# Attention with two gated layers on one core: conversion buffers moved into idle attention tiles, unit 8 eight positions later

## The chip, the core and the metric

The program runs on one core of a Trainium2 chip. The metric is device time in microseconds (us) of one execution. The core has five instruction streams: TensorE (PE; its weight loads stand apart as PEld), VectorE (DVE), ScalarE (ACT), GpSimd (POOL) and SyncE (SP), which here issues every DMA. SBUF is the on-chip memory that tiles live in, PSUM the one that TensorE writes.

## The reference, cut to what matters

```python
# q, k, v: [4, 8, 576, 64]; out_d attends over means of 4 rows, out_local over rows nearer than 4
out_d = sm_attn(q_d, k_d, v_d)
out_up = np.repeat(out_d, 4, axis=2)
mask = np.abs(pos[:, None] - pos[None, :]) < 4
scores = np.where(mask, scale * np.matmul(q, k.transpose(0, 1, 3, 2)), -1e9)
x = out_up + np.matmul(softmax(scores), v)            # then [2304, 512]
x = (silu(x @ w_gate) * (x @ w_val)) @ w_out          # d_ff = 1536
h = x @ w_in                                          # d_ff = 2048
out = (np.maximum(h, 0) + alpha * np.minimum(h, 0)) @ w_out2
```

The weights are handed over as 64-bit floats and are read as pairs of 32-bit words.

## The kernel before, in words

**Attention** is cut into 32 units (n = 0 to 31): four pairs of heads for each of eight blocks of 288 tokens. A unit transposes q and k (`a_T`), multiplies the scores into PSUM (`a_QK`, L335), takes the exponential and normalises (`a_EXP`, `a_NRM`; L419 transposes the local weights into a block-diagonal tile `bd`), and multiplies with v (`a_PV`, L431). The sum goes through ACT (L454), DVE (`xf`, L455), ACT (`xh`, L459) and POOL (`xl`, L460) into a high and a low half. The first layer's products of a block read `xh` and `xl` of its four units, the last unit's in the last three of the twelve products of a column tile. v is first copied in DRAM into overlapping windows (`stage`, L250: tensor `vwin`), from which `a_load_w` reads. Units 0 to 7 (`NPRO=8`) come ahead of the first layer's loop, the others are spread over it.

**Weights.** The first layer has 12 column tiles j, each with three slots g, v and o (gate, value, out). `w_load` (L100) brings a raw tile of 512 KB into a slot of pool `wp`; `w_split` (L124) converts it and writes the result, two 32-bit halves, into the same slot. A conversion is an ACT pass (L129), a second ACT pass on the top bytes (L137), a DVE pass (L139) that joins both, an ACT rounding (L142) and a subtraction for the low half (L143, on POOL here). It needs two scratch tiles, `st` and `sk`. Before, the first 30 conversions take both from three slots that rotate, o10, g11 and v11 (`st_slots`, L160); the last six take `st` from pool `hp_` and have no `sk`: then two DVE passes (L131, L132) stand in for L137 and L139.

**Slots shared with attention.** The slots of j = 4 to 11 first hold tiles of units 0 to 7 (`pslot`, L162): q and v of units 0 to 3 in g4 to g5, their work tiles `qs` in v5 to v6, their k in o6 to o7 (then q and v of units 4 to 7), `vd` in g8 to g9 (then `qs` of units 4 to 7; unit 7 has g9), and the block-diagonal tiles of units 0 to 3 in v9, o9, g10 and v10. Units 4 to 7 use those same four again. A raw tile can be loaded only when its slot's last reader is done.

**Order.** Each engine executes a fixed order that a list scheduler has worked out beforehand: program order is the priority, and of what it believes ready the first by priority is taken, also far ahead of its place. `tc.issue_after(x)` puts instructions behind x in their queue. The queue of SP is in order: a DMA that waits holds up those behind it.

**The loop** goes over 8 blocks and 12 column tiles, i = 12 blk + j. For each i it has gate products (`m_g`), value products (`m_v`) and out products of the i before (`m_y`), twelve matmuls each; after each of the three stands a position, 3i, 3i+1, 3i+2, at which steps of attention are hung (`at`, L724). Unit n of 8 and more multiplies its scores at p = OFF + 9(n - 8) and its values at p + 11 (L746 to L752), with OFF = 25. The loads of j = 4 to 9 and of unit 8 are placed ahead of the loop (L713 to L716), those of j = 10 and 11 and the copies `stage(2)`, `stage(3)` in block 0 when the tenth column tile has been handed to conversion (L773 to L779); `stage(2)` and `stage(3)` stand behind the DMA of o11, whose slot nothing else uses, `stage(1)` and unit 8's loads behind that of o7.

Of the kernel before, what the change touches and what calls it, by code (L numbers as in the profile page):

```python
# [8 lines left out]
F32 = mybir.dt.float32  # L9
# [7 lines left out]
DRAM = bass.MemoryType.DRAM  # L17


K = dict(kdP=0, qdP=0, dnP=2, ldn=9, lo='asvw0123', NPRO=8, c=5, a1=1, a2=0, OFF=25, oT=3, oE=3, oP=5, oV=11, vd1=2, vd2=1, pre=(1, 1, 0, 0), lo1=0, lo2=1, nst=3, nrm=0, sub=0, nrm1=0, sub1=0, qtA=0, ldw=1, xl1=0, ly=4, l2=3, st2=2, early=1, w2p=1, la=0, bdV=0, sp=9, s2=0, s3=0, gj=7, gs=1, vr=0, kc=0, gD=(0, 0, 0, 0, 0, 0), gP=(0, 2, 8, 8, 0, 0), gA=(0, 0, 0, 0, 0, 0))  # L20


@with_exitstack
def attn_moe_moe2_kernel(
# [13 lines left out]
    nc = tc.nc  # L38
    B, H, S, D = q.shape
# [6 lines left out]
    NP = H // 2  # L46
# [69 lines left out]
    def st_tile():  # L116
        c = stc[0]
        stc[0] += 1
        if c >= 3 * NEARLY:
            return stp[0].tile([128, 512], F32, tag="st", name="st", bufs=stn[0]), None  # L120
        t = wp.tile([128, 2, 512], F32, tag=st_slots[c % len(st_slots)], name="st2")
        return t[:, 0], t[:, 1]

    def w_split(slot, eng):  # L124
        t = raw.pop(slot)
# [23 lines left out]
    kds = {}  # L149
    vss = {}  # L150
    vds = {}
    bds = [ap_.tile([128, 2, NW, 128], F32, name=f"bd{i}", bufs=1) for i in range(NBD)]

    def coords(n):
        blk, hp = divmod(n, NP)
# [1 line left out]
        return b, half, hp, blk  # L157

    order = [f"{kind}{j}" for j in range(F1 - 8, F1) for kind in "gvo"]
    st_slots = order[5 * NP:][:K["nst"]]  # L160
    NEARLY = F1 - 2
    pslot = {(what, n): order[4 * i + n] for i, what in enumerate(("qv", "qs", "kn", "vd", "bd")) for n in range(NP)}  # L162
    for n in range(NP):
        pslot["qv", n + NP] = pslot["kn", n]
        pslot["qs", n + NP] = pslot["qs" if K["vr"] else "vd", n]
    NPRO = K["NPRO"]
    srs = [ap_.tile([128, 8], F32, name=f"sr{i}", bufs=1) for i in range(4)]

# [25 lines left out]
    def a_load(n):  # L194
        b, half, hp, blk = coords(n)
        h0, t0 = 2 * hp, half * HB
        d = hu[n] = {}
        if n >= NPRO:

            loads = [("qn", q, HB, t0)]  # L200
            if half == 0:
                loads.insert(0, ("kn", k, S, 0))
            for tag, src, rn, r0 in loads:
                t = d[tag] = ap_.tile([128, rn], F32, tag=tag, name=tag, bufs=1)
                for i in range(4):
                    nc.sync.dma_start(
                        out=t[32 * i:32 * (i + 1)].rearrange("r (m c) -> r m c", c=32),
                        in_=src[b, h0 + i // 2, r0:r0 + rn, 32 * (i % 2):32 * (i % 2 + 1)].rearrange("(m r) c -> r m c", r=32))
            return
        if half == 0:  # L210
            kn = d["kn"] = at_(n, [QB, 6, 2, D], "kn")
            for h in range(2):
                nc.sync.dma_start(out=kn[:, :, h], in_=k[b, h0 + h].rearrange("(r p) c -> p r c", p=QB))
        t = at_(n, [128, 2 * NW * 2 * D], "qv").rearrange("p (a w h c) -> p a w h c", a=2, w=NW, h=2)
        d["vw"] = t[:, 1]
        qn = d["qn"] = t[:QB, 0]
        for h in range(2):
            nc.sync.dma_start(out=qn[:, :, h], in_=q[b, h0 + h, t0:t0 + HB, :].rearrange("(r p) c -> p r c", p=QB))
# [18 lines left out]
    def a_load_w(n):  # L237

        b, half, hp, blk = coords(n)
        if n < NP:  # L240
            pbd[n] = at_(n, [128, 2, NW, 128], "bd")
            (nc.vector if K["bdV"] else nc.gpsimd).memset(pbd[n], 0.0)
        if n >= NPRO:
            hu[n]["vw"] = ap_.tile([128, NW, 2, D], F32, tag="vw", name="vw", bufs=NVW)
        t = hu[n]["vw"]
        for h in range(2):
            w0 = ((b * H + 2 * hp + h) * 2 + half) * NW * 128
            nc.sync.dma_start(out=t[:, :, h], in_=vwin[w0:w0 + NW * 128, :].rearrange("(w p) c -> p w c", p=128))
# [143 lines left out]
    def a_NRM(n):  # L392
        d = hu[n]
        sm, loc, sr = d["sm"], d["loc"], d["sr"]
        s4 = sr[:, 0:6].rearrange("p (h w) -> p h w", h=2)
        if not d["la"]:
            nc.vector.tensor_reduce(out=s4, in_=loc, axis=AX.X, op=ALU.add)
        if not d["act"]:
            nc.vector.reduce_sum(sr[:72, 6:8], sm[:72, :, LW:SW], axis=AX.X)
        nc.vector.tensor_scalar_add(out=sr, in0=sr, scalar1=1e-9)  # L400
        nc.vector.reciprocal(out=sr, in_=sr)
        nrm = K["nrm1" if n < NPRO else "nrm"]
        if nrm == 2:
            for h in range(2):
                for w in range(NW):
                    nc.scalar.mul(out=loc[:, h, w], in_=loc[:, h, w], mul=sr[:, NW * h + w:NW * h + w + 1])
        else:
            (nc.vector if nrm else nc.gpsimd).tensor_tensor(out=loc, in0=loc, in1=s4.unsqueeze(3).to_broadcast([128, 2, NW, SWIN]), op=ALU.mult)
        dn = n < 2 * NP and K["dnP"]
        if dn == 2:  # L410
            for h in range(2):
                nc.scalar.mul(out=sm[:72, h, LW:SW], in_=sm[:72, h, LW:SW], mul=sr[:72, 6 + h:7 + h])
        else:
            (nc.gpsimd if dn else nc.vector).tensor_tensor(out=sm[:72, :, LW:SW], in0=sm[:72, :, LW:SW],
                                in1=sr[:72, 6:8].unsqueeze(2).to_broadcast([72, 2, SD]), op=ALU.mult)
        d["bd"] = pbd[n % NP] if n < NPRO else bds[n % NBD]
        for i in range(NS):
            ps = slice(SWIN * i, SWIN * (i + 1))
            nc.vector.transpose(out=d["bd"][ps, :, :, SWIN * i:SWIN * (i + 1)], in_=loc[ps])  # L419
# [62 lines left out]
    def load1(j):  # L482
        for kind in "gvo":
            w_load(kind, j, f"{kind}{j}")
# [145 lines left out]
    if True:  # L630
# [26 lines left out]
                                fill=NEG, base=SUB + 2, channel_multiplier=0)  # L657
        for i in range(NS):
            nc.gpsimd.tensor_copy(mask[SWIN * i:SWIN * (i + 1)], tmp[:, :, i])
        for t in bds:  # L660
            nc.gpsimd.memset(t, 0.0)
        pstack = ExitStack()
        pgv = pstack.enter_context(tc.tile_pool(name="pgv", bufs=1, space=PSUM))
        P = [ATT, Y[0], Y[1], pgv.tile([128, 2, 512], F32, name="gv")]
# [39 lines left out]
            a_all(n, P[n % NP % 3])  # L704
        preps(K["pre"][3])
        def load8():
            if B > 1:
                stage(1)
            a_load(NPRO)
            a_load_v(NPRO)  # L710
            a_load_w(NPRO)

        for j in range(4, F1 - 2):  # L713
            load1(j)
        with tc.issue_after(wdma[f"o{K['gj']}"]):
            load8()  # L716
        for b in range(2, B):
            if K["gs"] == 0:
                stage(b)
        nc.sync.dma_start(out=alpha_sb, in_=alpha.rearrange("(j p) -> p j", p=128))  # L720

        ev = {}
# [1 line left out]
        def at(pos, fn):  # L724
            ev.setdefault(pos, []).append(fn)

        def a_pre(n):
            a_T(n, ATT)
            a_vd(n)
            if n + 1 < NHU:  # L730
                a_load(n + 1)
                a_load_v(n + 1)
# [4 lines left out]
                a_load_w(n + 1)  # L737

        OFF = K["OFF"]
        at(0 if NPRO == NP else OFF - 7, lambda: a_pre(NPRO))  # L740
        for n in range(NPRO, NHU):
            if n < 2 * NP:
                c = K["c"]
# [15 lines left out]
        for i, (blk, j) in enumerate(fts):  # L759
            if blk == NB1 - 1 and j == 0:  # L760
                assert not ev, ev.keys()
                astack.close()
                side2 = ctx.enter_context(tc.tile_pool(name="p2a", bufs=1, side="right"))
                stp[0] = side2
                attstack.close()
                pa2 = ctx.enter_context(tc.tile_pool(name="pa2", bufs=1, space=PSUM, side="right"))
                HT += GV[0], GV[1], *[pa2.tile([128, 512], F32, name=f"h{e}") for e in range(2)]
                stn[0] = K["st2"]
            if blk == 0:
                while pc[0] <= min(j + K["early"], F1 - 1):  # L770
                    prep1(pc[0])
                    pc[0] += 1
                    if pc[0] == NEARLY:  # L773
                        load1(F1 - 2)
                        load1(F1 - 1)
                        if K["gs"]:
                            with tc.issue_after(wdma[f"o{F1 - 1}"]):
                                for b in range(2, B):
                                    stage(b)  # L779
            m_g(blk, j)  # L780
            run(3 * i)
            m_v(blk, j)
            run(3 * i + 1)
            if i > 0:
                m_y(*fts[i - 1])
            run(3 * i + 2)
            if blk == NB1 - 1:
                load2(j)
                if j >= K["l2"]:
                    prep2(j - K["l2"])  # L790
                if j == K["ly"]:
                    load_y(0)
# [52 lines left out]
```

## Time and profile before

| | us |
|---|---|
| median of 3 runs (1015.98 to 1018.08) | 1017.56 |
| the profiled execution | 1017.97 |
| its span, first to last instruction | 1015.9 |
| TensorE busy in the span | 969.7 |
| ScalarE, VectorE, GpSimd busy | 306.8, 478.9, 383.5 |

The profiled execution has 2.1 us around its span. The matmuls of a column tile follow each other every 0.13 us, although each is shown with 0.29 us, since they overlap. Idle time of TensorE is what to look for; the clock that it was granted stands beside it, as a share of 2.4 GHz.

### The profile page before, as it was taken

What the parts mean: (1) busy time and instruction counts of PE and PEld (TensorE: products, weight loads), DVE (VectorE), ACT (ScalarE), POOL (GpSimd) and SP (SyncE); (2) the same over time, 40 slices, a digit from 0 to 9 for tenths busy, and PEclk for the clock granted to TensorE, in tenths of its full rate; (3) what the DMA queues carried; (4) which work ended last, traced back from release to release, by engine and by line L of the source; (5) the groups of instructions that cost most, each with busy time, mean ns of one, the idle gap of its engine ahead of it and who ended that gap; (6) DMA issues with size and microseconds to landing.
All of it is one profiled execution on the core that took longest, in us unless ns stands there. A gap on an engine that the chain in (4) does not pass through costs nothing.

```text
span 1015.9 us, 19233 instructions
## 1 busy us (share of the span) xinstructions
PE 969.7 (95%) x7760; PEld 865.3 (85%) x7760; DVE 478.9 (47%) x1015; ACT 306.8 (30%) x690; POOL 383.5 (38%) x492
## 2 busy tenths in 40 slices
PE   5489789999999999999999999999999999999998
PEld 4379679999999999999999998888888888888897
DVE  5577864555444555444532769622222322322232
ACT  3869632222221322222323556312111101211111
POOL 5868763234322344222223435624223322322222
PEclk9999899999999999999999999999999999999999
DMA  8998741132111321110103883102000100100010
GB/s 202 290 315 283 184 93 27 35 73 59 38 46 21 76 50 41 40 26 18 43 9 116 282 254 122 42 1 63 22 0 21 52 1 1 42 11 1 0 43 22
DMA packets 135894, 77.81 MB, mean 77 GB/s; under 512 B 97406, under 2 KB 127102, under 8 KB 135038
## 3 DMA queue, kind: packets, MB, share of 16 engines
q1 hardware_dynamic: 135804, 76.58, 27.0%
q8 instruction: 60, 0.98, 0.4%
q14 instruction: 30, 0.25, 0.1%
HBM read 67.12 MB, written 15.73 MB: 82 GB/s over the span
## 4 chain that ended last, share of the span: by engine, by line
PE 82%; SPq 4%; DVE 4%; DMA 3%; POOL 3%; issue 2%; ACT 2%; POOLq 0%; DVEq 0%; ACTq 0%
PE y L610 7%; PE y L612 6%; PE y L611 6%; PE g L473 6%; PE v L474 6%; PE v L473 6%; PE v L475 6%; PE g L474 6%; PE g L475 6%; PE y L473 4%; PE y L475 4%; PE y L474 4%; PE h L473 3%; PE h L475 3%; PE h L474 3%
## 5 line engine op out<-in xcount | busy, mean ns | idle before, releaser
L598 POOL TENSOR_TENSOR gl<-t,gh 128x512 fp32r<-128x512 f32 (+1 forms) x80 | 97.0, 1214 | 250.9 <-ACT gh L597 244.4
L597 ACT CAST gh<-t 128x512 fp32r<-128x512 f32 (+1 forms) x80 | 46.2, 578 | 278.7 <-DVE t L594 239.2
L473 PE MATMUL g<-xh,w 128*128 128x288 f32 x384 | 117.4, 306 | 10.0 <-DVE u L513 4.4
L475 PE MATMUL g<-xh,w 128*128 128x288 f32 x384 | 115.1, 300 | 1.9 <-POOL w L143 1.8
L473 PE MATMUL v<-xh,w 128*128 128x288 f32 x384 | 116.0, 302 | 0.6 <-ACT w L142 0.4
L474 PE MATMUL v<-xl,w 128*128 128x288 f32 x384 | 115.3, 300 | 0.0
L474 PE MATMUL g<-xl,w 128*128 128x288 f32 x384 | 115.0, 300 | 0.0
L474 PE MATMUL y<-pl,w 128*128 128x288 f32 x384 | 113.8, 298 | 1.3 <-POOL pl L523 1.2
L475 PE MATMUL v<-xh,w 128*128 128x288 f32 x384 | 113.8, 296 | 0.6 <-POOL w L143 0.6
L610 PE MATMUL y<-w,gh 128*128 128x512 f32 x288 | 113.2, 393 | 1.0 <-ACT sy L542 1.0
L475 PE MATMUL y<-ph,w 128*128 128x288 f32 x384 | 113.0, 296 | 0.0
L611 PE MATMUL y<-w,gh 128*128 128x512 f32 x288 | 112.8, 392 | 0.0
L612 PE MATMUL y<-w,gl 128*128 128x512 f32 x288 | 112.0, 392 | 0.0
L513 DVE SCALAR_TENSOR_TENSOR u<-u,g 128x288 f32<-128x288 f32 x96 | 43.3, 451 | 144.1 <-ACT u L512 144.1
L473 PE MATMUL y<-ph,w 128*128 128x288 f32 x384 | 111.0, 301 | 0.2 <-ACT ph L522 0.2
L523 POOL TENSOR_TENSOR pl<-u,ph 128x288 fp32r<-128x288 f32 x96 | 79.8, 832 | 59.4 <-ACT ph L522 58.6
L143 POOL TENSOR_TENSOR w<-st,w 128x512 fp32r<-128x512 f32 x52 | 70.2, 1356 | 60.7 <-ACT w L142 60.5
L473 PEld LDWEIGHTS g<-xh,w 128*128 128x128 f32 x384 | 73.5, 191 | 12.9 <-DVE u L513 5.7
L592 DVE TENSOR_SCALAR t<-h,alpha 128x512 f32<-128x512 f32 (+1 forms) x40 | 27.9, 697 | 110.7 <-PE h L475 109.5
L512 ACT ACTIVATE u<-g 128x288 f32<-128x288 f32 x96 | 39.4, 410 | 122.8 <-PE g L475 121.3
L475 PEld LDWEIGHTS g<-xh,w 128*128 128x128 f32 x384 | 73.7, 192 | 2.7 <-POOL w L143 2.4
L473 PEld LDWEIGHTS v<-xh,w 128*128 128x128 f32 x384 | 72.8, 190 | 2.3 <-DVE u L519 1.0
(190 smaller groups left out, 2143.4 us busy)
## 6 DMA issues: line engine op xcount, KB each, us to landing
raw<-in_moe_w_out_dram SPq DMA_DIRECT2D x28, 512.0 KB
raw<-in_moe_w_in_dram SPq DMA_DIRECT2D x16, 512.0 KB
raw<-in_moe_w_gate_dram SPq DMA_DIRECT2D x12, 512.0 KB
raw<-in_moe_w_val_dram SPq DMA_DIRECT2D x12, 512.0 KB
vw<-vwin SPq DMA_DIRECT2D x48, 96.0 KB
out_dram<-os SPq DMA_DIRECT2D x18, 256.0 KB
sy<-y SPq DMA_DIRECT2D x16, 256.0 KB
y<-ys SPq DMA_DIRECT2D x14, 288.0 KB
```

What stands on the lines that cost most here:

```text
L143: eng.tensor_sub(w[:, 1], st, f32(w[:, 0]))
L473: nc.tensor.matmul(o, lhi, rhi, start=first, stop=False)
L474: nc.tensor.matmul(o, lhi, rlo, start=False, stop=False)
L475: nc.tensor.matmul(o, llo, rhi, start=False, stop=last)
L512: nc.scalar.activation(out=u, in_=GV[0][:, :HB], func=AF.Tanh, scale=0.5)
L513: nc.vector.scalar_tensor_tensor(out=u, in0=u, scalar=1.0, in1=GV[0][:, :HB], op0=ALU.add, op1=ALU.mult)
L523: nc.gpsimd.tensor_sub(pl, u, f32(ph))
L597: nc.scalar.copy(out=gh[:, :n], in_=t[:, :n])
L598: nc.gpsimd.tensor_sub(gl[:, :n], t[:, :n], f32(gh[:, :n]))
L610: nc.tensor.matmul(o, gh[:, ms], ohi, start=(j == 0), stop=False)
L611: nc.tensor.matmul(o, gh[:, ms], olo, start=False, stop=False)
L612: nc.tensor.matmul(o, gl[:, ms], ohi, start=False, stop=(j == F2 - 1))
```

## The change

All 36 conversions of the first layer take `st` and `sk` from the pools of attention and of the first layer: of three conversions in a row the first two use tag `st` of `hp_` (two buffers), the third the tile `bd` of pool `ap_`; `sk` lies in `vd`, `kn` and a new tile `sk` of `ap_`. So slots o10, g11 and v11 are free of scratch, and units 4 to 7 get block-diagonal tiles of their own there and in o11, with a memset each. All raw tiles of j = 4 to 11 are loaded in one row. `load8` (unit 8's block-diagonal tile with its memset, `stage(1)`, unit 8's loads, `stage(2)` and `stage(3)`) is called when the last column tile has been handed to conversion, its DMAs behind that of o11. OFF goes from 25 to 33, the first step of unit 8 from position 18 to 31.

```diff
-K = dict(... OFF=25, ...)
+K = dict(... OFF=33, ...)
...
     def st_tile():
         c = stc[0]
         stc[0] += 1
-        if c >= 3 * NEARLY:
+        if c >= 3 * F1:
             return stp[0].tile([128, 512], F32, tag="st", name="st", bufs=stn[0]), None
-        t = wp.tile([128, 2, 512], F32, tag=st_slots[c % len(st_slots)], name="st2")
-        return t[:, 0], t[:, 1]
+
+        if c % 3 == 2:
+            st = ap_.tile([128, 512], F32, tag="bd", name="st", bufs=1)
+        else:
+            st = hp_.tile([128, 512], F32, tag="st", name="st", bufs=NST)
+        return st, ap_.tile([128, 512], F32, tag=("vd", "kn", "sk")[c % 3], name="sk", bufs=1)
...
-    bds = [ap_.tile([128, 2, NW, 128], F32, name=f"bd{i}", bufs=1) for i in range(NBD)]
+    bds = []
...
-    st_slots = order[5 * NP:][:K["nst"]]
-    NEARLY = F1 - 2
...
         pslot["qs", n + NP] = pslot["qs" if K["vr"] else "vd", n]
+        pslot["bd", n + NP] = order[5 * NP + n]
...
-        if n < NP:
+        if n < NPRO:
             pbd[n] = at_(n, [128, 2, NW, 128], "bd")
             (nc.vector if K["bdV"] else nc.gpsimd).memset(pbd[n], 0.0)
...
-        d["bd"] = pbd[n % NP] if n < NPRO else bds[n % NBD]
+        d["bd"] = pbd[n] if n < NPRO else bds[n % NBD]
...
-        for t in bds:
-            nc.gpsimd.memset(t, 0.0)
...
         def load8():
-            if B > 1:
+            bds.append(ap_.tile([128, 2, NW, 128], F32, tag="bd", name="bd", bufs=1))
+            nc.gpsimd.memset(bds[0], 0.0)
+            with tc.issue_after(wdma[f"o{F1 - 1}"]):
                 stage(1)
-            a_load(NPRO)
-            a_load_v(NPRO)
-            a_load_w(NPRO)
-
-        for j in range(4, F1 - 2):
+                a_load(NPRO)
+                a_load_v(NPRO)
+                a_load_w(NPRO)
+                for b in range(2, B):
+                    stage(b)
+
+        for j in range(4, F1):
             load1(j)
-        with tc.issue_after(wdma[f"o{K['gj']}"]):
-            load8()
...
-        at(0 if NPRO == NP else OFF - 7, lambda: a_pre(NPRO))
+        at(0 if NPRO == NP else OFF - 2, lambda: a_pre(NPRO))
...
                     pc[0] += 1
-                    if pc[0] == NEARLY:
-                        load1(F1 - 2)
-                        load1(F1 - 1)
-                        if K["gs"]:
-                            with tc.issue_after(wdma[f"o{F1 - 1}"]):
-                                for b in range(2, B):
-                                    stage(b)
+                    if pc[0] == F1:
+                        load8()
```

## Rows read from the trace of the kernel before

**Rows 1.** The page, parts 1 and 2: TensorE's busy time; its granted clock.

```profile
PE 969.7 (95%) x7760; PEld 865.3 (85%) x7760; DVE 478.9 (47%) x1015; ACT 306.8 (30%) x690; POOL 383.5 (38%) x492
...
PEclk9999899999999999999999999999999999999999
```

**Rows 2.** Busy time by stretch: engines' us (instructions), granted clock, DMA share, GB/s.

```profile
54.00:69.00 15.00, 10.64 (x203) 8.77 (x202) 13.40 (x40) 10.73 (x33) 11.02 (x19) 0.92 0.98 330
...
66.50:104.00 37.50, 37.44 (x368) 35.87 (x369) 27.93 (x56) 31.39 (x73) 28.65 (x28) 0.95 0.88 296
104.00:118.40 14.40, 11.14 (x121) 9.77 (x120) 12.66 (x21) 10.70 (x22) 11.86 (x12) 0.98 0.75 185
118.40:124.80 6.40, 4.17 (x16) 3.35 (x16) 6.37 (x12) 1.68 (x5) 5.13 (x6) 0.50 0.71 161
124.80:149.00 24.20, 21.23 (x232) 18.65 (x233) 19.40 (x40) 10.40 (x23) 16.50 (x22) 1.00 0.43 91
```

**Rows 3.** Timeline, TensorE: start, length, line, operation; in brackets idle before and releaser.

```profile
106.23 0.40 PE L473 MATMUL g<-xh,w 128*128 128x288 f32 x1 [1.06 <-DVE u L513]
...
118.47 0.61 PE L473 MATMUL g<-xh,w 128*128 128x288 f32 x1 [2.18 <-ACT w L142]
...
121.15 0.61 PE L475 MATMUL g<-xh,w 128*128 128x288 f32 x1 [1.83 <-POOL w L143]
...
137.62 0.40 PE L473 MATMUL v<-xh,w 128*128 128x288 f32 x1 [0.45 <-ACT w L142]
...
140.34 0.40 PE L475 MATMUL v<-xh,w 128*128 128x288 f32 x1 [0.59 <-POOL w L143]
...
143.12 0.40 PE L473 MATMUL g<-xh,w 128*128 128x288 f32 x1 [0.94 <-DVE u L513]
```

**Rows 4.** Timeline, DMA issues of SP: start, and length until the group's last issue.

```profile
55.27 0.52 SPq L257 DMA_DIRECT2D vwin<-in_v_dram  x1
55.89 0.54 SPq L106 DMA_DIRECT2D raw<-in_moe_w_val_dram  x1
...
83.30 12.37 SPq L104 DMA_DIRECT2D raw<-in_moe_w_out_dram  x2
95.73 0.53 SPq L257 DMA_DIRECT2D vwin<-in_v_dram  x1
...
106.35 0.45 SPq L106 DMA_DIRECT2D raw<-in_moe_w_gate_dram  x1
...
121.13 0.35 SPq L104 DMA_DIRECT2D raw<-in_moe_w_out_dram  x1
...
122.92 0.41 SPq L106 DMA_DIRECT2D raw<-in_moe_w_val_dram  x1
```

**Rows 5.** DMA issues by source and size: the large copies of v.

```profile
vwin<-in_v_dram SPq DMA_DIRECT2D x2, 1536.0 KB
```

**Rows 6.** Timeline, ScalarE: first passes of two conversions.

```profile
69.96 0.67 ACT L129 ACTIVATE st<-raw 128x512 f32<-128x512 f32 x1
...
116.27 0.67 ACT L129 ACTIVATE st<-raw 128x512 f32<-128x512 f32 x1
```

**Rows 7.** Timeline, GpSimd: the low half of unit 7's result.

```profile
101.44 1.28 POOL L460 TENSOR_TENSOR xl<-qs,xh 128x288 fp32r<-128x288 f32 x1
```

**Rows 8.** Operations by line: count, ns (min/median/max), first and last start.

```profile
L137 ACT ACTIVATE st<-raw x30: 641/660/697, 28.8 to 116.8; 128x512 int32<-128x512 uint8 x30
...
L242 POOL MEMSET bd<- x4: 738/740/742, 0.9 to 3.2; 128x768 f32 x4
```

**Rows 9.** Timeline: values of units 11 and 12, unit 11's low half, block 2's first product.

```profile
197.03 0.67 PE L450 MATMUL att<-bd,vw 128*64 128x96 f32 x12
...
200.37 0.81 POOL L460 TENSOR_TENSOR xl<-xf,xh 128x288 fp32r<-128x288 f32 x1 [2.19 <-ACT xh L459]
...
209.27 0.30 PE L473 MATMUL g<-xh,w 128*128 128x288 f32 x1
...
213.92 0.67 PE L450 MATMUL att<-bd,vw 128*64 128x96 f32 x12
```

More of the change, by code (lines that the diff above doesn't have):

```diff
@@ L17 @@
 DRAM = bass.MemoryType.DRAM
-K = dict(kdP=0, qdP=0, dnP=2, ldn=9, lo='asvw0123', NPRO=8, c=5, a1=1, a2=0, OFF=25, oT=3, oE=3, oP=5, oV=11, vd1=2, vd2=1, pre=(1, 1, 0, 0), lo1=0, lo2=1, nst=3, nrm=0, sub=0, nrm1=0, sub1=0, qtA=0, ldw=1, xl1=0, ly=4, l2=3, st2=2, early=1, w2p=1, la=0, bdV=0, sp=9, s2=0, s3=0, gj=7, gs=1, vr=0, kc=0, gD=(0, 0, 0, 0, 0, 0), gP=(0, 2, 8, 8, 0, 0), gA=(0, 0, 0, 0, 0, 0))
+K = dict(kdP=0, qdP=0, dnP=2, ldn=9, lo='asvw0123', NPRO=8, c=5, a1=1, a2=0, OFF=33, oT=3, oE=3, oP=5, oV=11, vd1=2, vd2=1, pre=(1, 1, 0, 0), lo1=0, lo2=1, nst=3, nrm=0, sub=0, nrm1=0, sub1=0, qtA=0, ldw=1, xl1=0, ly=4, l2=3, st2=2, early=1, w2p=1, la=0, bdV=0, sp=9, s2=0, s3=0, gj=7, gs=1, vr=0, kc=0, gD=(0, 0, 0, 0, 0, 0), gP=(0, 2, 8, 8, 0, 0), gA=(0, 0, 0, 0, 0, 0))
 @with_exitstack
@@ L706, in load8 @@
         def load8():
-            if B > 1:
+            bds.append(ap_.tile([128, 2, NW, 128], F32, tag="bd", name="bd", bufs=1))
+            nc.gpsimd.memset(bds[0], 0.0)
+            with tc.issue_after(wdma[f"o{F1 - 1}"]):
                 stage(1)
-            a_load(NPRO)
-            a_load_v(NPRO)
-            a_load_w(NPRO)
-        for j in range(4, F1 - 2):
-            load1(j)
-        with tc.issue_after(wdma[f"o{K['gj']}"]):
-            load8()
-        for b in range(2, B):
-            if K["gs"] == 0:
-                stage(b)
+                a_load(NPRO)
[4 more added lines that the diff above has]
+        for j in range(4, F1):
+            load1(j)
         nc.sync.dma_start(out=alpha_sb, in_=alpha.rearrange("(j p) -> p j", p=128))
@@ L772, in attn_moe_moe2_kernel @@
                     pc[0] += 1
-                    if pc[0] == NEARLY:
-                        load1(F1 - 2)
-                        load1(F1 - 1)
-                        if K["gs"]:
-                            with tc.issue_after(wdma[f"o{F1 - 1}"]):
-                                for b in range(2, B):
-                                    stage(b)
+                    if pc[0] == F1:
+                        load8()
             m_g(blk, j)
```

## The prediction

> **What bounds the kernel now.** I read the page first, then busy time by stretch, then the timelines of the engines in the stretches that are not full. TensorE is busy for 969.7 of 1015.9 us and its clock is full but for slices near the start [rows 1], so the time can fall only where TensorE idles or runs at the lower clock. Between 66.5 and 104 us it is full, 37.44 of 37.50 us, and so it is again after 149. What this change can reach lies between: 3.26 us idle up to 118.4, 2.23 up to 124.8, 2.97 up to 149, together 8.46 us; and from 118.4 to 124.8 the clock is 0.50, which is 1.2 instead of 2.4 GHz, so that the 4.17 busy us of that stretch could have been 2.1 [rows 2]. The ceiling is thus 8.46 + 2.1 = 10.6 us.
>
> The timeline names the waits [rows 3]. At 118.47 TensorE has waited 2.18 us for a rounded gate weight, at 121.15 another 1.83 for its low half, then come 0.45, 0.59 and 0.94 us at the end of block 0; 1.06 us at 106.23 waits for DVE. They are waits for conversions, and the DMA queue says why those are late [rows 4]. The first v copy goes out at 55.27, right among the raw tiles, a value tile behind it at 55.89; then two out tiles hold SP from 83.30 to 95.67, since unit 7 still has the slot of the second (o7); a copy and unit 8's loads follow, and only at 106.35 the gate tile that is needed next. That is g9, since its slot holds unit 7's `qs`, which POOL reads until 102.72 [rows 7]; its conversion begins at 116.27 [rows 6]. The last raw tiles, for slots that served as scratch, go out at 121.13 and 122.92 [rows 4], and those are the conversions that the three late waits want.
>
> **The change, part by part.**
>
> *Scratch and raw tiles.* There were three scratch pairs in rotation and there are three now, so the pace is as before: 0. With scratch out of o10, g11 and v11, and the bd tiles of units 0 to 3 no longer held by units 4 to 7, only o7, g9 and o11 still wait for unit 7. All other raw tiles can go ahead of 95 us, in the place of the v copies, which now stand behind o11. The conversions wanted at 137.62, 140.34 and 143.12 then no longer depend on loads at 121 us and later: 0.45 + 0.59 + 0.94 = 1.98 us gone. Bounds: nothing, if conversions are late for want of ScalarE, and the whole 2.97 us idle of that stretch [rows 2]. I take 2.0. What is late next there is ScalarE itself.
>
> *g9.* It still needs unit 7's last read, at 102.72 [rows 7], and so cannot be issued much sooner than that, 3.6 us before its 106.35 [rows 4]. But o11 needs only unit 7's value products, so it comes first, and behind it now go all three copies, not one. Two of them have 1536 KB each [rows 5] and the third is of like size, some 4.6 MB; at the 330 GB/s of the stretch that copied before [rows 2] that is 14 us from 96 on. The value tile issued at 55.89 behind a copy had its first conversion pass at 69.96 [rows 4, 6], 14 us later. So g9 may land at 110 to 113 all the same. What it gains is the work in front of it on ScalarE, since the other conversions are done by then. Its wait and the half clock behind it make 2.18 + 1.83 + 2.1 = 6.1 us. Bounds 0 and 6.1; I take 2.5, nearer to the low end because its load is moved by 3.6 us at most.
>
> The Trainium skill, "DMA: Bandwidth & Descriptors", section "Two DMAs through the same engine are not ordered", says that descriptors of one queue on one engine start in order; by that g9 lies behind all the copies, as the 14 us of that value tile suggest, though no row shows its landing by itself. If small transfers were instead served beside large ones, g9 would land near 105, its 6.1 us would go whole, and the sum would be 1010.9.
>
> *The wait at 106.23*, 1.06 us, comes from DVE behind ScalarE, which is full of conversions: between 0 and 1.06, half taken, 0.5.
>
> *Added work.* Six conversions get a second ACT pass of 0.66 us [rows 8], 4.0 us on ScalarE, in exchange for one of two DVE passes. ScalarE is busy 10.40 of 24.2 us at the end of block 0 [rows 2], which hides it; if the six move ahead of 104, where it is busy 31.39 of 37.5, 4.0 us of delay is what it costs at worst, and then TensorE has its earlier backlog to do. Four memsets come and one moves, 0.74 us each [rows 8], 3 us of POOL, ready from the start; the first conversion pass on top bytes is at 28.8, so they hide in the wait for the first weights. Taken as 0.
>
> *Unit 8.* Its k and v tiles now lie in the last conversions' scratch, so they load some 25 us later than now, right behind the copy at 95.73 [rows 4]. POOL's v sums and the score products queue behind those loads; the block that needs unit 8's group starts near 200, and four units at 17 us each fit. 0 taken, 3 us if TensorE has to stand for it once.
>
> *Eight positions later.* Between the values of units 11 and 12, nine positions, lie 213.92 - 197.03 = 16.89 us [rows 9], so a position is 1.88 us and eight are 15.0. Unit 11's low half is ready at 201.18, block 2's first product starts at 209.27 [rows 9]: 8.1 us to spare before, 6.9 too few after. The first nine products of the tile do not need unit 11, and the second of the last three, which reads the low half, comes 1.3 us after the first; so 5.6 us are to be filled. There is work: nine value products (1.2), the out products of the block before (1.6), unit 11's own values (0.9), score products of the next units (1.0) and transposes (0.6), in sum 5.3. This happens at block 2 to 7, six times; the last has no unit behind it, whose scores would be in the way. Bounds: 0 each, and 5.6 each or 33.6 in all if TensorE filled in nothing. I take 0.3, what is left after filling, five times: 1.5 us. It is nearest to what the timeline shows for the ordinary steps, where values of one unit run inside the products of a block without idle time.
>
> *Sum*, against the profiled execution's 1017.97 (0.41 above the median of the runs): 1017.97 - 2.0 - 2.5 - 0.5 + 1.5 = 1014.5.
>
> **The rivals.**
>
> *The block ends stall* (slower). The chain from values to low half takes 3.5 us, 197.70 to 201.18 [rows 9], and the values themselves must wait until the next unit's scores have been read. If only the value and out products fill, 2.8 of 5.6 us are open at each end; I price it at 2.0, five times, 10 us. It decides at 1.0 us per end, where it eats the 5.0 gained. For it: at 121.15 TensorE stood 1.83 us instead of taking other work [rows 3], and a wait of about 2 us was followed by the half clock [rows 2]. Against: the planner sees the dependency and has work at hand. 1017.97 - 5.0 + 10 = 1023.
>
> *The copies keep g9 as late as it was* (no change): the change does not do for g9 what it does for the others. Then only the late waits go: 1017.97 - 2.0 + 1.5 = 1017.5. For it speaks the row at 55.89, against it the work that is gone from in front of g9.
>
> *All the loss goes*: g9 slips in before the copies or unit 7 ends sooner. 1017.97 - 10.6 + 1.5 = 1008.9. Against it: unit 7 has no new help.
>
> **How the numbers follow.** A measurement of this kernel tells about 0.2% from no change, 2.0 us: faster is below 1015.5, slower above 1019.6. Forecast 0.36, block ends 0.27, g9 as late 0.24, all gone 0.13. Of the forecast 0.32 is faster and 0.04 same; of the block ends 0.25 slower and 0.02 same; of g9 as late 0.03 faster, 0.17 same and 0.04 slower; the last is faster whole. Faster 0.48, same 0.23, slower 0.29. The range runs from 1008, where the ceiling of the gain lies, to 1023, where half of the block-end case is left out. The likeliest case alone has 1012 to 1016.
>
> **What would show it.** Right: the copies of v in one row after the raw tiles; no wait for a conversion after g9; g9's wait under 3 us; waits of a few tenths for `xl` at the first gate products of blocks 2 to 7. Wrong: waits of over 1 us for `xl` at those six places, or a clock of 0.50 behind them; ScalarE late at the end of block 0; TensorE waiting on unit 8's k; or SP issuing a copy ahead of a raw tile that could go.

## The result, and the profile after

The changed kernel takes 1023.49 us (median of 4 runs, 1021.08 to 1024.14), the kernel before beside it 1017.03 (1015.98 to 1018.08): a ratio of 1.0060, 95% interval 1.0045 to 1.0075. It is **slower** by some 6 us; 1014.5 was predicted. Its profiled execution took 1023.53 us with a span of 1021.7. The code below `st_tile` stands three or four lines further down: L473 to L475, the layer's products, are now L476 to L478, the scores L345 and L349 are L348 and L352, and `xl` is written at L463.

The page, parts 1 and 2, answers to [rows 1]:

```profile
PE 972.2 (95%) x7760; PEld 866.5 (85%) x7760; DVE 486.3 (48%) x1009; ACT 310.8 (30%) x696; POOL 388.3 (38%) x496
...
PEclk9999999999999999999999999999999999999999
```

TensorE executes the same 7760 instructions and is busy 2.5 us longer, in a span that is 5.8 us longer. So only part of the loss is idle time, and no slice of the span shows a lower clock than before [rows 1]. Busy time by stretch, with the columns of [rows 2]:

```profile
66.50:104.00 37.50, 31.49 (x324) 29.36 (x323) 26.46 (x53) 31.02 (x73) 27.63 (x29) 0.95 0.70 232
81.00:92.00 11.00, 5.94 (x31) 5.47 (x31) 8.04 (x15) 9.67 (x24) 10.76 (x11) 0.84 0.65 218
104.00:118.40 14.40, 12.83 (x92) 12.12 (x92) 6.80 (x13) 12.14 (x25) 9.26 (x8) 1.00 1.04 361
118.40:124.80 6.40, 5.67 (x41) 5.26 (x40) 5.07 (x6) 6.06 (x13) 5.73 (x5) 1.00 0.23 42
124.80:149.00 24.20, 22.74 (x255) 21.11 (x254) 13.35 (x31) 6.94 (x16) 13.72 (x19) 1.00 0.54 111
```

Where the change was to gain, it gained: from 104 to 149 us TensorE idles 1.57 + 0.73 + 1.46 = 3.76 us in place of 8.46, and the clock is full where it was 0.50 [rows 2]. But ahead of it a stretch that was full now has a hole: 6.0 us idle between 66.5 and 104, of which 5.06 lie between 81 and 92, at a mean clock of 0.84. The timeline of TensorE, columns as in [rows 3]:

```profile
81.74 0.40 PE L476 MATMUL y<-ph,w 128*128 128x288 f32 x1 [0.74 <-DVE qs L458]
...
85.23 0.53 PE L476 MATMUL y<-ph,w 128*128 128x288 f32 x2 [1.65 <-ACT ph L525]
...
88.44 0.61 PE L477 MATMUL y<-pl,w 128*128 128x288 f32 x1 [2.68 <-POOL pl L526]
...
114.49 0.40 PE L476 MATMUL g<-xh,w 128*128 128x288 f32 x1 [0.91 <-ACT w L146]
...
115.56 0.40 PE L476 MATMUL v<-xh,w 128*128 128x288 f32 x1 [0.54 <-ACT w L146]
...
121.39 0.37 PE L476 MATMUL g<-xh,w 128*128 128x288 f32 x1 [0.67 <-DVE u L516]
...
128.10 0.40 PE L478 MATMUL g<-xh,w 128*128 128x288 f32 x1 [0.47 <-POOL w L147]
...
159.92 0.44 PE L429 MATMUL att<-ident,sm 72*72 72x72 f32 x4 [1.44 <-DVE xf L458]
...
282.19 0.40 PE L477 MATMUL g<-xl,w 128*128 128x288 f32 x1 [0.77 <-POOL xl L463]
...
422.04 0.41 PE L477 MATMUL g<-xl,w 128*128 128x288 f32 x1 [0.86 <-POOL xl L463]
```

The first wait is for DVE; the next two are for the layer's own activations, `ph` from ScalarE and `pl` from GpSimd: both engines have conversions in front of them (GpSimd is busy 10.76 of 11 us). The waits for weights shrank from 2.18 and 1.83 us to 0.91, 0.54 and 0.47. The one at 159.92 comes with unit 8: the next unit's transposes wait until DVE has read unit 8's result. The last two are ends of blocks. SP's DMA issues answer to [rows 4]:

```profile
85.00 14.47 SPq L104 DMA_DIRECT2D raw<-in_moe_w_out_dram  x3
99.52 0.55 SPq L260 DMA_DIRECT2D vwin<-in_v_dram  x1
100.12 1.09 SPq L209 DMA_DIRECT2D qn<-in_q_dram  x2
101.31 0.41 SPq L106 DMA_DIRECT2D raw<-in_moe_w_gate_dram  x1
101.77 4.41 SPq L209 DMA_DIRECT2D qn<-in_q_dram  x2
106.23 3.28 SPq L260 DMA_DIRECT2D vwin<-in_v_dram  x3
```

The gate tile g9 goes out at 101.31, 5 us sooner than before, behind one copy of v and two loads of unit 8; the other copies go out from 106.23 on.

After 165 us the long stalls end and the loss begins. I timed each block by the end of its last out product in the timeline. Blocks 2 to 5, which have 2944 TensorE instructions in both kernels, last 67.73, 68.55, 67.73 and 68.88 us before, 272.9 together, and 69.77, 69.99, 69.77 and 70.10 after, 279.6: **6.7 us, the size of the loss**. The other four blocks, taken together, differ by 0.2 us. Only a quarter of the 6.7 us is idle time. Busy time from 220 to 480 us, before and then after:

```profile
220.00:480.00 260.00, 260.00 (x2836) 247.51 (x2834) 130.17 (x344) 64.71 (x172) 84.01 (x148) 1.00 0.19 42
```

```profile
220.00:480.00 260.00, 258.37 (x2693) 243.81 (x2693) 132.10 (x331) 65.17 (x169) 83.24 (x145) 1.00 0.19 42
```

TensorE is shown busy for 260.00 and 258.37 of 260 us at the full clock; only the number in brackets tells that it gets 143 instructions fewer done. 90 of them are local scores (768 against 678 in the stretch), which follow each other every 0.015 us on average; 31 are products of the layer, worth 31 x 0.13 = 4.0 us, and 22 are other products of units. The missing 1.6 us are two waits for `xl`, whose start for unit 11 went from 200.37 [rows 9] to 209.68. For the rest, look at how the timeline goes through one unit's 52 score products:

```profile
304.81 0.29 PE L478 MATMUL y<-ph,w 128*128 128x288 f32 x1
305.04 0.26 PE L348 MATMUL att<-kT,qT 64*32 64x32 f32 x6
305.23 0.40 PE L476 MATMUL g<-xh,w 128*128 128x288 f32 x1
...
306.79 0.29 PE L478 MATMUL g<-xh,w 128*128 128x288 f32 x1
307.01 0.57 PE L348 MATMUL att<-kT,qT 64*32 64x32 f32 x42
307.51 0.47 PE L352 MATMUL att<-kd,qd 64*72 64x144 f32 x4
307.91 0.40 PE L476 MATMUL v<-xh,w 128*128 128x288 f32 x1
```

Six scores stand ahead of a gate tile and 46 behind it. I call each such passage a visit. The first product of a visit starts 0.22 us after the layer's product before it, where two of the layer's are 0.13 apart, and the way back costs as much again. Blocks 2 to 5 have 25 visits to the scores before and 32 after, for 16 units. The transposes have 16 visits in both. The values have 16 before and 20 after: in each of the four blocks one unit's 20 value products are cut in two, here 18 and 2:

```profile
218.03 0.47 PE L449 MATMUL att<-pt,vs 72*64 72x72 f32 x8
218.33 0.66 PE L453 MATMUL att<-bd,vw 128*64 128x96 f32 x10
...
223.69 0.29 PE L478 MATMUL y<-ph,w 128*128 128x288 f32 x1
223.91 0.38 PE L453 MATMUL att<-bd,vw 128*64 128x96 f32 x2
224.22 0.40 PE L476 MATMUL g<-xh,w 128*128 128x288 f32 x1
```

### The profile page after: what moved, and what is told of

Same layout as the page of the kernel before. It is cut to its first block, busy times and chain, and to the rows that moved or that the text cites. A ratio compares the mean times of both kernels' runs of the same rounds, so it can differ in the third digit from the quotient of the medians.

```text
span 1021.7 us, 19195 instructions
## 1 busy us (share of the span) xinstructions
PE 972.2 (95%) x7760; PEld 866.5 (85%) x7760; DVE 486.3 (48%) x1009; ACT 310.8 (30%) x696; POOL 388.3 (38%) x496
## 4 chain that ended last, share of the span: by engine, by line
PE 79%; DMA 5%; DVE 4%; SPq 4%; POOL 3%; issue 2%; ACT 2%; POOLq 0%; DVEq 0%; ACTq 0%
PE y L613 6%; PE y L615 6%; PE y L614 6%; PE g L476 6%; PE v L476 6%; PE g L477 6%; PE g L478 5%; PE v L478 5%; PE v L477 5%; PE y L477 4%; PE y L478 4%; PE y L476 4%; PE h L476 3%; PE h L478 3%; PE h L477 3%
## 5 line engine op out<-in xcount | busy, mean ns | idle before, releaser
L476 PE MATMUL g<-xh,w 128*128 128x288 f32 x384 | 120.6, 314 | 10.0 <-DVE u L516 4.9
L476 PE MATMUL v<-xh,w 128*128 128x288 f32 x384 | 117.0, 305 | 0.6 <-ACT w L146 0.5
L478 PE MATMUL g<-xh,w 128*128 128x288 f32 x384 | 114.5, 298 | 0.6 <-POOL w L147 0.5
L478 PE MATMUL v<-xh,w 128*128 128x288 f32 x384 | 113.3, 295 | 0.0
L478 PE MATMUL y<-ph,w 128*128 128x288 f32 x384 | 112.6, 296 | 0.0
L476 PE MATMUL y<-ph,w 128*128 128x288 f32 x384 | 109.5, 298 | 2.4 <-ACT ph L525 1.6
L147 POOL TENSOR_TENSOR w<-st,w 128x512 fp32r<-128x512 f32 x52 | 73.3, 1419 | 47.0 <-ACT w L146 46.8
L476 PEld LDWEIGHTS g<-xh,w 128*128 128x128 f32 x384 | 72.7, 189 | 16.3 <-DVE u L516 7.5
L476 PEld LDWEIGHTS v<-xh,w 128*128 128x128 f32 x384 | 72.4, 188 | 5.7 <-issue 3.9
L477 PEld LDWEIGHTS y<-pl,w 128*128 128x128 f32 x384 | 72.7, 189 | 4.8 <-POOL pl L526 4.6
L477 PEld LDWEIGHTS g<-xl,w 128*128 128x128 f32 x384 | 73.0, 190 | 3.5 <-POOL xl L463 2.3
```

Of the source, the lines that this page charges most:

```text
L147: eng.tensor_sub(w[:, 1], st, f32(w[:, 0]))
L476: nc.tensor.matmul(o, lhi, rhi, start=first, stop=False)
L477: nc.tensor.matmul(o, lhi, rlo, start=False, stop=False)
L478: nc.tensor.matmul(o, llo, rhi, start=False, stop=last)
```

## The experiments

Two theories stood at first. **A**: the eight positions cost the 7 us of blocks 2 to 6. **B**: the loss is the hole at 81 to 92 us and unit 8's lateness. Every run had its own runs of the kernel before beside it, so the ratios are what to compare; a hundredth of a per cent is 0.1 us. The edits are cut to what changes, with numbers in place of the names of constants; "visits" alone are those to the scores in blocks 2 to 5.

**1. The shift alone** (on the kernel before)

```diff
-OFF=25
+OFF=33
```

> The kernel before with one number changed: every unit from 8 on stands eight positions later (OFF 33 for 25); buffers, raw tiles and copies as before. Theory A, that the eight positions are what the change lost: the blocks from 2 to 6 last 1.0 to 2.0 us longer each, as in the changed kernel (69.8 to 70.0 us for one where the kernel before has 67.7 to 68.6), PE goes to the score products in more visits per block (9 for 5), and the time is 5 to 9 us over before, about 1024 us. Theory B, that the loss lies in blocks 0 and 1 (conversions that ScalarE and POOL do ahead of the softmax's work) and the shift is harmless: within 2 us of before, 1015 to 1019 us.

1023.88 us, ratio 1.0068 (1.0053 to 1.0083). Blocks 2 to 5 last 69.77, 70.25, 69.77 and 70.11 us with 32 visits, as in the changed kernel; from 81 to 92 us TensorE is busy 11.00 of 11 us. The shift makes the whole loss by itself. A holds, and B falls as the explanation of the total; the hole is then paid for by the gains beside it.

**2. The shift given back by spacing units 7 apart** (on the changed kernel)

```diff
-p = OFF + 9 * (n - 8)
+p = max(25 + 9 * (n - 8), OFF + 7 * (n - 8))
```

> The changed kernel, but from unit 8 on the units stand 7 positions apart, not 9, until each is back where the kernel before has it (unit 12 is the first): blocks 0 and 1 stay as changed, blocks 2 to 6 get the places of before. Theory A: 5 to 7 us faster than the changed kernel, 1016 to 1018 us, no wait for an xl over 0.5 us at the ends of blocks 2 and 4, and visits to the score products at about 5 per block. Theory B: no difference from the changed kernel beyond 2 us, 1021 to 1025 us.

With 7 positions, units 8 to 11 have their block-diagonal tile overwritten by the next unit's softmax before their values are multiplied, so that those values use other weights; the amount of work is the same. 1022.4 us, ratio 1.0047 (1.0035 to 1.0060), so 1.3 us gained, not 5 to 7: a miss in the time. The blocks tell why: 3 to 6 last 68.56, 67.72, 68.88 and 65.36 us, what they last before to 0.01 us, but block 2 takes 77.08, since it holds 94 TensorE instructions more and waits of 2.10 and 0.88 us.

**3. Copies of k and v among the raw tiles** (on the changed kernel)

```diff
-for b in range(2, B): stage(b)      # in load8, behind o11
-for j in range(4, F1): load1(j)
+load1(4)
+with tc.issue_after(wdma["g4"]):
+    for b in range(2, B): stage(b)
+for j in range(5, F1): load1(j)
```

> The changed kernel, but the six stages of copies of k and v go back among the raw tiles, behind raw tile g4, not after the last of them, so that the raw tiles from o4 on land some us later. If the new stall of PE at 81 to 92 us (5.94 us busy of 11) is there because all the raw tiles come so early that ScalarE and POOL have conversions in front of ph and pl: that stall shrinks by 2 us or more, and the waits for w after g9 grow to what before had (about 4 us); the time stays within 2 us of the changed kernel's 1023.5. If the stall has another cause (the conversions' buffers), PE's busy time at 81 to 92 us stays within 0.5 us of 5.94, and the waits at g9 still grow: 1 to 3 us slower.

1022.25 us, ratio 1.0042 (1.0030 to 1.0054). Busy time by stretch:

```profile
81.00:92.00 11.00, 10.56 (x89) 9.56 (x88) 8.20 (x17) 11.00 (x26) 8.36 (x9) 1.00 1.07 364
104.00:118.40 14.40, 9.88 (x61) 8.23 (x60) 7.22 (x12) 12.76 (x26) 9.78 (x9) 1.00 0.21 52
```

The hole is gone, 10.56 us busy for 5.94, and 2.95 us of it come back at 104 to 118.4. So the hole is made by raw tiles that land sooner and are converted ahead of `ph` and `pl`; where the loads stand decides where TensorE waits more than how much.

**4. Low halves of the o conversions on VectorE** (on the changed kernel)

```diff
-lo1=0
+lo1=1
```

> The changed kernel with the low halves of the conversions of the o matrices (and of what goes with them) on VectorE in the place of POOL. If POOL's queue (10.76 us busy of 11 at 81 to 92 us) is what makes PE wait for pl there: PE's busy time at 81 to 92 us rises from 5.94 us to 8 or more, the half clock there goes, and the time falls by 2 to 5 us, to 1019 to 1021 us. If ScalarE is (ph came late before pl did): under 1 us of gain in that stretch. Theory A, with the loss in blocks 2 to 6: these keep their length, so the time stays over 1018 us in either case.

1022.82 us, ratio 1.0051 (1.0038 to 1.0063): a miss. The hole has 6.80 us busy, its waits merged into one:

```profile
86.94 0.40 PE L477 MATMUL y<-pl,w 128*128 128x288 f32 x1 [4.20 <-POOL pl L526]
```

GpSimd is still busy 10.94 of the 11 us, with `xl` and gate and value conversions, and the blocks keep their 69.8 us.

**5. Back to the old places by units 8 apart** (on the changed kernel)

```diff
-p = OFF + 9 * (n - 8)
+p = max(25 + 9 * (n - 8), OFF + 8 * (n - 8))
```

> The changed kernel, but from unit 8 on the units stand 8 positions apart, not 9, until each is back at its place of before (unit 16, position 97, is the first): blocks 0 and 1 keep the change, block 2 comes in between, blocks 3 to 6 get the places of before, with every unit done before the next begins to write its tiles. Theory A, the places of the units cost 1.2 to 2.0 us per block: blocks 3 to 6 last what they do before (68.55, 67.73, 68.88 and 65.36 us) and the time is 4 to 6 us under the changed kernel, 1017.5 to 1019.5 us. Theory B, the loss is in blocks 0 and 1: 1021 us or more.

1015.59 us, ratio 0.9986 (0.9974 to 0.9998). Blocks 3 to 6 are those of before once more: 68.56, 67.72, 68.88 and 65.36 us. The places of the units alone turn the loss into a small gain.

**6. OFF 24 on the kernel before**

```diff
-OFF=25
+OFF=24
```

> The kernel before with every unit from 8 on one position earlier (OFF 24 for 25). 24 and 33 differ by one whole unit's spacing of 9, so the units lie to the feed-forward products exactly as in the changed kernel, only each with nine positions in hand before its block begins. If the place within the block is what costs (more visits of PE to the scores): blocks 2 to 5 last 69 to 70 us and the time is 1021 to 1024 us. If it is that a unit ends on the very position at which its block begins, so that its own products are what PE has left and xl comes late: blocks as before, 67.7 to 68.9 us, no wait for xl over 0.3 us, and 1016 to 1019 us.

1021.54 us, ratio 1.0039 (1.0027 to 1.0051): one position *earlier* costs 4 us. Blocks 2 to 5 last 69.98, 68.86, 69.98 and 68.83 us with 38 visits, and no wait for `xl` shows. Here a unit has nine positions in hand: the last of a block ends nine positions ahead of the block, where with OFF 33 it ends at the very position at which the block begins. So blocks can be slow without lateness.

**7. OFF 32 on the changed kernel**

```diff
-OFF=33
+OFF=32
```

> The changed kernel with the units from 8 on one position earlier (OFF 32 for 33), so that the last of a block is done one position before the block begins. If ending on the block's first position is what costs: the waits for xl (0.77 and 0.86 us) go and blocks 2 to 5 shorten by 0.5 to 1.5 us each, 1018 to 1021 us. If lateness in general costs, smoothly: about an eighth of the 7 us, 0.5 to 1 us, 1022 to 1023 us.

1015.54 us, ratio 0.9985 (0.9975 to 0.9994): better than either expectation. Blocks of 67.60, 68.57, 67.60 and 68.01 us, 16 visits, the least that sixteen units can have; the values still have 20.

**8. OFF 29 on the kernel before**

```diff
-OFF=25
+OFF=29
```

> The kernel before with every unit from 8 on four positions later (OFF 29 for 25), half of the shift. If lateness costs smoothly: half of the 6 us of the whole shift, 1020 to 1022 us. If only the last positions cost (the unit that ends where its block begins): 1016 to 1019 us, blocks 2 to 5 at 67.7 to 68.9 us. If the place within the block costs: any value, and the number of visits to the scores per block (5 to 8 before, 7 to 9 after) goes with the time.

1011.95 us, ratio 0.9945 (0.9931 to 0.9959), faster than before by 5.6 us; 16 visits to the scores and 16 to the values, blocks of 67.54 to 67.57 us. Half of the shift gains where the whole of it loses, which led to the next two.

**9 and 10. OFF 26 and 27 on the kernel before**

> The kernel before with the units from 8 on one position later (OFF 26 for 25). The positions run gate, value, out, and the units stand 9 apart, so OFF modulo 3 says behind which of the three products every unit's scores stand: 0 behind the gate products, 1 behind the value products, 2 behind the out products. So far 24 and 33 (0) were slow, 25 (1) between, 29 (2) fastest. Theory C, that this is what sets the time of blocks 2 to 5: 26 goes with 29, blocks of 67.5 to 67.7 us, 4 visits of PE to the scores per block, 1011 to 1013.5 us. Theory D, that the number of positions in hand does it, with a best value near 29: 26 lies by 25, 1016 to 1017.5 us.

> The kernel before with the units from 8 on two positions later (OFF 27 for 25); 27 leaves 0 modulo 3, as 24 and 33 do. Theory C: slow, blocks 2 to 5 of 68.8 to 70 us, 8 or more visits to the scores per block, 1020 to 1022.5 us, slower than the kernel with 26 by 8 us for one position. Theory D: faster than 26, 1013 to 1016 us.

26: 1012.7 us, ratio 0.9957 (0.9944 to 0.9969), 16 visits, the four blocks 67.84 us on average, but 66.46 to 68.67 one by one, where 67.5 to 67.7 was expected. 27: 1019.9 us, ratio 1.0031 (1.0021 to 1.0042), 36 visits, 69.22 us on average. One position, over 7 us: theory C holds, D falls.

**11. OFF 32 on the kernel before**

> The kernel before with OFF 32: scores behind the out products as with 29, one position in hand as in the changed kernel with OFF 32 (1015.5 us), so that the two differ in the rest of the change alone (buffers, raw tiles in a row, copies behind them, unit 8's loads). If that rest is worth nothing, as 1023.9 (shift alone) against 1023.5 us (all) says: 1014.5 to 1016.5 us. If it is a gain that the shift hid: 1018 us or more. If it is a loss: 1012 to 1013.5 us, as with 29.

1013.31 us, ratio 0.9964 (0.9950 to 0.9978). At OFF 32 the rest of the change thus costs 0.9985 against 0.9964, some 2 us; at OFF 33 it gains 1.0068 against 1.0060, some 0.8. With intervals of over 1 us to either side of each ratio, neither is told well from nothing.

**12. OFF 32 and the copies among the raw tiles** (on the changed kernel; runs 3 and 7 together)

> The changed kernel with OFF 32 and the copies of v and k behind raw tile g4 as in the run with the copies among the raw tiles, which was 1.2 us under the changed kernel. If the two add up: 1014 to 1015 us. If the loads of unit 8, wanted one position sooner, now stand behind later raw tiles and PE waits for them at its values: 1016 us or more.

1011.87 us, ratio 0.9951 (0.9939 to 0.9964): better than the sum. Against run 11 this leaves the rest of the change, with the copies back, about 1 us ahead, within the intervals.

**13 to 16. One step of a unit moved**, in 13 and 14 on the kernel before with OFF 27, in 15 and 16 on the changed kernel as it is. Scores alone (13, 15), values alone (14, 16):

```diff
-at(p, lambda n=n: a_QK(n, ATT))
+at(p - 1, lambda n=n: a_QK(n, ATT))
```

```diff
-oV=11
+oV=10
```

> The kernel before with OFF 27 (1019.9 us), with one step of each unit from 8 on moved: its score products one position earlier, behind the out products in place of the gate products; transposes, softmax and values stay. If the broken visits to the scores carry the price: 4 visits per block in place of 8 to 10, blocks 2 to 5 about 1.4 us shorter (5 visits by some 0.3 us), 67.6 to 68.2 us, and 1012.5 to 1015 us. If the place of another step carries it: visits may fall, but blocks stay over 68.8 us and the time over 1018 us.

> The kernel before with OFF 27, with the value products of each unit from 8 on one position earlier, behind the value products of the layer, and nothing else moved. If the visits to the scores carry the price: these stay at 8 to 10 per block and the time within 1.5 us of 1019.9 us. If the place of the values does: 1013 to 1016 us.

> The changed kernel as it is (OFF 33), with the score products alone one position earlier. If the visits carry most of the price and the unit's end on the block's first position the rest: 4 visits per block in place of 7 to 9, blocks 2 to 5 at 68.2 to 68.7 us (from 69.8 to 70.1), waits for xl still there, 1016 to 1019 us. If the block's end is most of it: blocks stay over 69.3 us and the time at 1021 us or more.

> The changed kernel as it is (OFF 33), with the value products alone one position earlier, so that a unit ends one position before its block begins. If the visits carry most: still 7 to 9 visits per block, the waits for xl shorter, 0.4 to 0.6 us off each block, 1019.5 to 1022 us. If the block's end is most of it: blocks of 68.5 us or less and under 1018 us.

| run | us | ratio (interval) | blocks 2 to 5, mean us | visits to the scores | to the values |
|---|---|---|---|---|---|
| 10: OFF 27 | 1019.9 | 1.0031 (1.0021 to 1.0042) | 69.22 | 36 | 16 |
| 13: scores earlier | 1011.8 | 0.9950 (0.9938 to 0.9962) | 67.52 | 16 | 16 |
| 14: values earlier | 1020.31 | 1.0034 (1.0022 to 1.0047) | 69.22 | 36 | 16 |
| the change, OFF 33 | 1023.49 | 1.0060 (1.0045 to 1.0075) | 69.91 | 32 | 20 |
| 15: scores earlier | 1016.2 | 0.9993 (0.9978 to 1.0009) | 68.01 | 16 | 20 |
| 16: values earlier | 1024.61 | 1.0071 (1.0058 to 1.0083) | 69.94 | 32 | 20 |

Moving the scores takes 6.8 and 7.6 us off the four blocks, moving the values nothing. In 13 the scores are whole; one unit's:

```profile
292.89 0.29 PE L475 MATMUL y<-ph,w 128*128 128x288 f32 x1
293.12 0.62 PE L345 MATMUL att<-kT,qT 64*32 64x32 f32 x48
293.67 0.47 PE L349 MATMUL att<-kd,qd 64*72 64x144 f32 x4
294.07 0.40 PE L473 MATMUL g<-xh,w 128*128 128x288 f32 x1
```

From the out product to the gate product it is 294.07 - 292.89 = 1.18 us. The broken passage above took 305.23 - 304.81 = 0.42 and 307.91 - 306.79 = 1.12, of which 0.13 would have passed between two products of the layer anyway: 0.23 us more, and the layer's next product comes 0.1 late as well (305.23 to 305.46). From 10 to 13 four blocks lose 276.9 - 270.1 = 6.8 us for 20 visits, **0.34 us a visit**. By that price, 9 visits between 25 and 16 are 3 us, where the four blocks of before and of run 13 differ by 272.9 - 270.1 = 2.8.

The same stretch from 220 to 480 us, run 10 and then run 13, and of both what stood ahead of the local scores (L345):

```profile
220.00:480.00 260.00, 260.00 (x2767) 245.62 (x2765) 137.00 (x342) 66.64 (x173) 84.83 (x148) 1.00 0.19 42
```

```profile
220.00:480.00 260.00, 260.00 (x2859) 249.20 (x2858) 135.32 (x346) 67.13 (x174) 86.02 (x150) 1.00 0.20 42
```

```profile
  issue: 5.6, 34
```

```profile
  issue: 2.6, 16
```

Both are busy 260.00 of 260 us; one gets 92 instructions more done, 48 small scores, 4 larger ones and 40 products of the layer (40 x 0.13 = 5.2 us). The second number of "issue" counts the visits within the stretch, 34 and 16, and each has 0.16 us ahead of it for which the profile names no other engine.

The visits to the values have a price too, which moving them by one position didn't touch, since it left their number as it was. Runs 13 and 15 both have 16 visits to the scores and no wait for `xl`; with 20 visits to the values in place of 16, the four blocks take 272.0 us in run 15 and 270.1 in run 13. On the kernel before it is 271.8 us in run 11 (20) and 270.2 in run 8 (16).

The 6.7 us of the change thus split, as an estimate, into 7 more visits to the scores (7 x 0.34 = 2.4 us), 4 more to the values (1.9, run 15 less run 13) and 1.6 us of waits for `xl`; 0.8 us are left over. The first part comes from the neighbour behind which the scores stand. The other two show only where a unit has one position in hand or none (OFF 32 and 33): no unit's values are cut in runs 6, 8, 9 and 10. So how late a unit comes has a share after all.

What the end on a block's first position does is told by 15 and 16. With the values earlier the waits for `xl` stay, where I had expected them to shrink, and the time is over the expected range; the waits from 205 to 560 us, in total, times, longest:

```profile
PE g L477 <- POOL xl L463: 1.7, 2, 0.9
```

With the scores earlier there is no such line, though I had expected the waits to stay. By these two runs the chain that ends in `xl` hangs on the scores, not on the position of the values.

## Why the prediction was wrong

**The step that failed is "Eight positions later"**, priced at 1.5 us; by run 1 it costs 1.0068, 6.9 us. I looked for idle time at the six block ends and asked whether TensorE would find work to fill them. That part was right in kind and near in size: it found work, and in blocks 2 to 5 the ends show 0.77 and 0.86 us of waiting for `xl`, 1.6 us. What I never priced is what the scheduled order itself costs. A shift by 8 is no multiple of 3, so every unit's scores moved from behind the value products to behind the gate products, and in blocks 2 to 5 they came in 32 visits for 25 (some 2.4 us); in the same blocks the values came in 20 visits for 16 (some 1.9 us). I had taken such steps as free because they "run inside the products of a block without idle time"; there is none in the rows, and it costs all the same.

**The rival "The block ends stall"** gave 1023 and the time came out at 1023.5, but not by its mechanism: it wanted about 2 us of waiting at each of five ends, and no such waits exist. Runs 6 and 10 have nine and six positions in hand and are slow all the same. The number was right by accident.

**Late conversions, -2.0:** the waits of 0.45, 0.59 and 0.94 us at the end of block 0 [rows 3] are gone, as forecast; 0.67 and 0.47 came in their place, which leaves 0.8 us.

**g9, -2.5:** more than I took, within my bounds. 2.18 + 1.83 us and the half clock became 0.91 + 0.54 at the full clock, some 4.7 of the 6.1. It was issued at 101.31 ahead of the large copies, which I had put in front of it, and before 102.72, where I had put its earliest time: GpSimd had unit 7's low half done at 100.99. That is the way of the rival "All the loss goes", not mine. So the wait under 3 us that I named came by another way. The rule of the Trainium skill, "DMA: Bandwidth & Descriptors", section "Two DMAs through the same engine are not ordered", that I weighed there was not put to a test.

**The wait at 106.23, -0.5:** gone whole.

**Added work, 0, and unit 8, 0:** these ate the gains. My bound of 4.0 us for conversions that move ahead of 104 was dismissed with TensorE's "earlier backlog"; it had none there, and idled 5.06 us at 81 to 92, most of it behind `ph` and `pl`. Late next was not ScalarE at the end of block 0 but ScalarE and GpSimd 50 us before it. From 149 to 165 us, where unit 8 comes in, TensorE was busy 16.00 us before and 13.32 after, 2.7 us more idle, close to my bound of 3.

**The sum** without the shift was thus to be -5.0 and came out between a gain of 0.8 (run 1 against the change) and a loss of 2 us (run 11 against run 7): 6.8 us saved from 104 to 149 (4.7 idle and 2.1 of half clock) and 1.9 by an earlier first product (46.5 for 48.4 us) stand against 6.0 and 2.7 lost beside them. Which sign it has is open, as is why the list scheduler cuts the scores in pieces where they hang behind gate or value products and leaves them whole behind out products. The runs show that it does and what it costs; they don't show the rule.

**Versions faster than both kernels** came out of it: the kernel before with OFF 29 (1011.95 us, ratio 0.9945) or with the scores alone moved (run 13, 0.9950), and the changed kernel with OFF 32 and the copies among the raw tiles (run 12, 0.9951). They are not told apart.

## What to carry to other kernels

Where an engine is shown full, count its instructions in a fixed stretch: 260.00 us busy hid a difference of 92 in 2859. When steps of one job are hung into the loop of another, a shift is two changes, how early the step comes and between which two neighbours it lands; try the neighbouring places one by one before asking about lateness. And a load that comes sooner is also work that comes sooner on the engines that convert it, so the stretch ahead of the repaired one has to be priced as well.

## What the hardware showed that was not expected

A switch of TensorE from the layer's products, which use 128 rows and 128 columns of it, to the local scores (64*32 in the rows) and back costs 0.3 us (0.34 a visit by runs 10 and 13), though no engine is waited for: the first score starts 0.23 us after the layer's last product (304.81 to 305.04), and the layer's second product behind a visit 0.23 us after its first (305.23 to 305.46), where 0.13 is the rule. The value products (72*64, 128*64) start 0.22 us behind the layer's too (223.69 to 223.91). The transposes of `sm`, 72*72, do not; run 15, timeline of TensorE:

```profile
298.23 0.29 PE L478 MATMUL y<-ph,w 128*128 128x288 f32 x1
298.36 0.41 PE L429 MATMUL att<-ident,sm 72*72 72x72 f32 x4
298.58 0.38 PE L476 MATMUL g<-xh,w 128*128 128x288 f32 x1
298.79 0.29 PE L477 MATMUL g<-xl,w 128*128 128x288 f32 x1
```

They start 0.13 us behind the layer's product, and the next product 0.22 us behind the first of four. So the way in is not slow by a change of operands or a short product as such. The way back is another matter: the layer's second product behind the transposes is late too, 0.21 us behind its first. The Trainium skill, "TensorEngine Tiling (Array Packing)", section "Key Properties", says that a change of the tiling mode, not of the tile alone, drains TensorE. The trace agrees for the way in, if 64*32 counts as a mode of its own and 72*72 runs in the mode of the full array; no run here took the drain apart from the rest of a visit. The prediction did not weigh that rule. Over the kernel it is about one per cent between two orders of the same work (run 6 against run 8, 1.0039 and 0.9945).
